# Gated attention and MLP on one core: the SBUF addresses of what TensorE reads

## The chip, the cores and the metric

One core of a Trainium2 chip runs the whole program. Its engines are TensorE (PE in the profile, with its weight loads apart as PEld), VectorE (DVE), ScalarE (ACT), GpSimd (POOL) and SyncE (SP), which issues the transfers here. The metric is the device time of one execution in microseconds, as the median of several runs. "Bytes modulo 512" below is the remainder of a tile's start address in its SBUF partition, the same in all 128 partitions.

## What is computed

Sequence 2048, width 512, 32 heads of 16, a causal window of 256 keys, an MLP of width 1792, and a gate that mixes both results:

```python
x = A_x                                            # [1, 2048, 512]
g = sigmoid((x * gate_w).sum(-1, keepdims=True))
qkv = x @ wqkv                                     # 32 heads of 16
p = softmax(where(0 <= i - j < 256, q @ k.T * 16 ** -0.5, -1e9))
a = (p @ v) @ wo
b = gelu(x @ w1 + b1) @ w2 + b2                    # tanh form
return g * a + (1 - g) * b
```

## The kernel before

The sequence is cut into NT = 4 tiles of T = 512 rows and 16 blocks of 128. Every dense product is made of three matmuls (`mm3`, L107 to L110): each operand is split into a high and a low part, and high by high, high by low and low by high are summed. Such a matmul reads 128 columns of weights and 512 columns of the other operand, in 4-byte elements.

The dense work is one generator, `dense()` (L896): `qkv(t)` for the four tiles (transposes of x at L261, then q and k at L294 and V at L334), `mlp(n)` for eight half-layers (first product "u", second product "y"), and `final(t)` (product "a" with `wo`).

Attention runs beside it from about 105 us on. For each unit of work the loop at L926 records: a matmul for the row maxima (L519, tile `sm`, weights from the stack `qd`, moving operand from the stack `kd`), one for the scores (L564, tile `st`, weights from the stack `ks`, moving operand from the stack `qs`), on every fourth block the products with V (L608, tiles `pv_st` and `pv_sm`, weights from `vbuf`, moving operand the probabilities `pt`), and then as much dense work as its estimate of the unit's time allows (`fill`, L907). So TensorE's queue alternates `sm`, `st` and about three dense matmuls. VectorE takes the row maxima (L524), ScalarE the exponentials (L586), GpSimd cuts the window's ends (L580) and writes the maxima into rows of `qs` (L546). The order of all five engines is written out by this loop (`manual_schedule`, L44), with a table of due times (`after`, L115); no scheduler moves anything afterwards. All transfers are issued by SP.

The tiles lie in SBUF in the order of their pools, and nearly fill it. From low to high addresses, with the start modulo 512 bytes:

| tiles | read by TensorE as | bytes modulo 512 |
|---|---|---|
| `qs`, `ks`, `qd`, `kd` (stacks of q and k, 16, 16, 16 and 12 KB) | scores and maxima; in `qkv(0)` to `qkv(2)` also x | 0 |
| `ident`, `x1`, `ya`, `xr` and other working tiles | transposes | 0 |
| `pt` (7 of 5 KB) | moving operand of L608 | 0 |
| `xt` (16 KB) | x of the MLP, x of `qkv(3)` | 0 |
| `w` (14 of 4 KB), `h` (7 of 4 KB) | weights and activations, high and low parts | 0 |
| `M`, `den`, `jm`, `b1c`, `cut`, `own`, `nil`, `nm` | `nil` only | various |
| `vbuf` (V, two halves, heads 68 bytes apart) | weights of L608 | 0 |

Inside a tile the matmuls start at multiples of 512 bytes, but for `qs` and `kd`, whose starts step by 64 columns (256 bytes), and `pt` (also 256). The stacks serve twice: `qkv_x` (L247) puts the transposed x of the tiles 0, 1 and 2 into the buffers of `ks`, `qd` and `qs` (L251 and L252), before attention needs them.

Of the kernel before, what the change touches and what calls it, by code (L numbers as in the profile page):

```python
# [9 lines left out]
F32 = mybir.dt.float32  # L10
F32R = mybir.dt.float32r
BF16 = mybir.dt.bfloat16
AF = mybir.ActivationFunctionType
ALU = mybir.AluOpType
# [3 lines left out]
S, D, F, H, DH, W = 2048, 512, 1792, 32, 16, 256  # L18
T = 512
NT = S // T  # L20
NB = T // 128
NC = D // 128
# [10 lines left out]
def gated_mix(ctx: ExitStack, tc: tile.TileContext, x, wqkv, wo, w1, b1, w2, b2, gate_w, out):  # L33
    nc = tc.nc
    x = x[0]
    out = out[0]

    cp = ctx.enter_context(tc.tile_pool(name="cp", bufs=1))
    sb = ctx.enter_context(tc.tile_pool(name="sb", bufs=1))
    cs = ctx.enter_context(tc.tile_pool(name="cs", bufs=1))  # L40
# [5 lines left out]
    def f32(ap):  # L46
        return ap.bitcast(F32)

    tt = cp.tile([128, 2 * RB, 32], F32, name="tt")
    mask = cp.tile([128, 320], BF16, name="mask")  # L50
    qs = cp.tile([128, 2, S], F32R, name="qs")
    ks = cp.tile([128, 2, 2, 2 * T], F32R, name="ks")
    qd = cp.tile([128, 2, 2, 2 * T], F32R, name="qd")
    kd = cp.tile([128, 2, 2, W + T], F32R, name="kd")

    idle = cs.tile([128, 320], BF16, tag="jm", bufs=1, name="idle")
    nc.gpsimd.memset(idle, 0.0)


    SQ = [dr.tile([H // NC, 16, 3, NC, T], F32, name=f"SQ{t}") for t in range(NT)]  # L60
# [12 lines left out]
    gwb = sb.tile([128, D], F32, tag="ya", bufs=2, name="gwb")  # L73
# [10 lines left out]
    for r in (0, 64):  # L84
        for e in (0, 1):
            v = cut[r:r + 64, e]
            nc.gpsimd.affine_select(out=v, in_=v, pattern=[[1 - 2 * e, 64]], compare_op=ALU.is_ge, fill=0.0,
                                    base=-e, channel_multiplier=2 * e - 1)

    own = cs.tile([128, 4], F32, name="own")  # L90
    nil = cs.tile([128, 1], F32, name="nil")
    nc.gpsimd.memset(nil, 0.0)
    nc.gpsimd.memset(own, 0.0)
    for s in (0, 1):
        for k in (0, 1):
            v = own[64 * s:64 * s + 4].rearrange("r (p s) -> r s p", s=2)[:, s]
# [1 line left out]
                                    fill=1.0, base=-k, channel_multiplier=1)  # L98
    nms = cs.tile([128, 2 * RB, 32], F32R, name="nm")
    nc.gpsimd.memset(f32(nms), 0.0)  # L100
    vbuf = cs.tile([128, 2, NB * 68 + 16], F32, name="vbuf")
    nc.gpsimd.memset(vbuf[:, :, NB * 68:], 0.0)
    z = cs.tile([128, S // 128], F32, name="z")
    g = cs.tile([128, S // 128], F32, name="g")
    g1 = cs.tile([128, S // 128], F32, name="g1")

# [8 lines left out]
    def after(ns, fn, *args):  # L115
        now[1] += 1
        heapq.heappush(todo, (now[0] + ns, now[1], fn, args))
# [7 lines left out]
    def tick(ns):  # L125
        now[0] += ns
        while todo and todo[0][0] <= now[0]:
            step_todo()
# [9 lines left out]
    def half_pt(name):  # L138

        if not spare:  # L140
            v = sb.tile([128, 2, 2, 320], F32, tag="pt", bufs=PTS, name=name)
            v = v.rearrange("p h a b -> p h (a b)")
# [104 lines left out]
    def qkv_x(t, b):  # L247

        if b == 0:
            if t < NT - 1:  # L250
                v = (ks.rearrange("p a b c -> p (a b c)"), qd.rearrange("p a b c -> p (a b c)"),  # L251
                     qs.rearrange("p a c -> p (a c)"))[t]  # L252
                v = v.rearrange("p (c s t) -> p c s t", c=NC, s=2)
            else:
                v = sb.tile([128, NC, 2, T], F32R, tag="xt", bufs=1, name=f"xt{t}")
            xts[t] = v
        xt = xts[t]
        xr = xrs[t, b]
        p = ps.tile([128, NC, 128], F32, tag="sm", bufs=3, name=f"xp{t}_{b}")
        for c in range(NC):  # L260
            nc.tensor.transpose(p[:, c], xr[:, c * 128:(c + 1) * 128], ident)  # L261
        tick(0 if t == 0 else 4 * 110)

        def hi():
            nc.scalar.activation(xt[:, :, 0, b * 128:(b + 1) * 128], p, AF.Copy)

        def lo():
            nc.vector.tensor_sub(xt[:, :, 1, b * 128:(b + 1) * 128], p,
                                 f32(xt[:, :, 0, b * 128:(b + 1) * 128]))
            done.add(("x", t, b))  # L270
        if t == 0:
            hi(), lo()
        else:
            after(100, hi), after(500, lo)

    def gate(t):
        for b in range(NB):
            after(1500 * b, gate_z, t, b)
        after(6500, gate_end, t)

    def gate_end(t):
        sl = slice(t * NB, (t + 1) * NB)
        nc.scalar.activation(g1[:, sl], z[:, sl], AF.Exp, scale=-1.0)
        nc.vector.tensor_scalar(g1[:, sl], g1[:, sl], 1.0, None, op0=ALU.add)
        nc.vector.reciprocal(g[:, sl], g1[:, sl])
        nc.vector.tensor_scalar(g1[:, sl], g[:, sl], -1.0, 1.0, op0=ALU.mult, op1=ALU.add)

    def gate_z(t, b):
        xr = xrs.pop((t, b))
        junk = sb.tile([128, D], BF16, tag="sq", bufs=2, name=f"xj{t}_{b}")  # L290
        nb = t * NB + b
        nc.vector.tensor_tensor_reduce(junk, xr, gwb, 1.0, 0.0, ALU.mult, ALU.add, z[:, nb:nb + 1])

    def qkv_qk(t, j):  # L294

# [198 lines left out]
    def load_qs(g_, c):  # L494
        ready(c, g_, 0)
        need(("v", NT - 2, NB - 1))
        for s in range(2):
            v = f32(qs[64 * s + 4:64 * s + 52, :, c * T:(c + 1) * T])
            nc.sync.dma_start(v, part(SQ[c], g_, s).rearrange("r (a c) -> r a c", a=2))
# [53 lines left out]
    def att_exp(g_, kb, i):  # L553
# [4 lines left out]
        if i == 0:  # L558
            pts[g_, kb] = sb.tile([128, 2, 2, 320], F32, tag="pt", bufs=PTS, name=f"pt{g_}_{kb}")
        pt = pts[g_, kb]  # L560
# [6 lines left out]
        n = 1 + (w == W + 64)  # L567
        late = g_ * NKB + kb >= NU - LEAD
        both = not late and kb % NB < NB - 1
# [22 lines left out]
    def att_pvs(u):  # L592

        g_, kb = divmod(u, NKB)
        c, k = divmod(kb, NB)
# [323 lines left out]

    NU = NG * NKB  # L920
    NQ = NG * NT
# [4 lines left out]
    for u in range(-LEAD, NU):  # L926
        m = u + LEAD
        gm, bm = divmod(m, NKB)
        step = STEP if u >= 0 else STEP0
        for i in range(4):  # L930
# [8 lines left out]
            for op, i in [(op, k) for k in pair for op in ORDER[:3]] + [("f", k) for k in pair]:  # L939
                if op == "s" and u >= 0:  # L940
                    att_exp(u // NKB, u % NKB, i)
                if op == "m" and m < NU:
# [5 lines left out]
        if m < NU and bm % RB == RB - 1:  # L948
            after(900, att_rows, gm, bm // RB)
        if m % NB == QAT % NB and QAT <= m < QAT + NKB:  # L950
            load_qs(0, (m - QAT) // NB)
# [18 lines left out]
WARM = (9, 4)  # L970
RB = 4
NKB = S // 128
PTS = 7
RAWS = 152000.0
PUT = 1200
# [44 lines left out]
```

## Time and profile before

| | |
|---|---|
| median of 3 runs | 750.84 us (750.7 to 752.2) |
| the profiled execution, its own time | 750.61 us |
| its span, from the first to the last instruction | 748.9 us |
| granted TensorE clock, mean | 1.000 |
| busy: PE, PEld, DVE, ACT, POOL | 98%, 81%, 70%, 56%, 50% |
| transfers | 172.12 MB, 230 GB/s over the span |

The table is from the page of the profile. Busy times of PE are those of overlapping matmuls: a matmul's recorded duration (about 0.39 us for 512 columns) is longer than the distance to the next one's start (0.23 us), since the next begins while the first drains. How much each matmul costs is therefore read from starts in the timeline, not from durations.

### The profile page before, as it was taken

The page shows a single profiled execution, that of the slowest core. Times are in us where ns is not written, and L with a number is a line of the kernel's source. Part 1 is how long each engine was busy: PE and PEld are TensorE (multiplying, and loading weights), DVE is VectorE, ACT ScalarE, POOL GpSimd, SP SyncE. Part 2 cuts the span into 40 slices and gives each one's busy share as a digit, 9 for nine tenths or more (in the row PEclk, how much of TensorE's full clock was granted, in tenths as well). Part 3 has the DMA queues.
Part 4 walks back from the last instruction along what each step waited for, and adds up shares of the span by engine and source line. Part 5 has one row for each costly group of instructions (what it writes and reads, how often), then busy time and mean ns, then how long its engine had stood idle before and what let it go on. Part 6 is the DMA issues. An engine that isn't in the chain of part 4 may idle for free.

```text
span 748.9 us, 17963 instructions
## 1 busy us (share of the span) xinstructions
PE 734.0 (98%) x6129; PEld 606.7 (81%) x6129; DVE 520.6 (70%) x1567; ACT 421.7 (56%) x972; POOL 372.4 (50%) x846
## 2 busy tenths in 40 slices
PE   9999999998999999999999999999999999999998
PEld 7888888876788888888887887888888888878787
DVE  4532325799768867986798689768867886784552
ACT  4434532358537845764695478447735853784541
POOL 4200000339756865876587567747765875630000
PEclk9999999999999999999999999999999999999999
DMA  9889798997995777799676989996799799438682
GB/s 316 329 268 407 257 392 277 273 312 182 273 251 133 172 229 211 176 227 249 164 174 152 241 215 230 259 235 155 171 268 244 180 238 239 136 88 262 217 287 106
DMA packets 179259, 172.12 MB, mean 230 GB/s; under 512 B 56672, under 2 KB 122976, under 8 KB 179168
## 3 DMA queue, kind: packets, MB, share of 16 engines
q1 hardware_dynamic: 179168, 170.97, 81.3%
q8 instruction: 49, 0.80, 0.5%
q14 instruction: 42, 0.34, 0.2%
HBM read 108.53 MB, written 62.39 MB: 228 GB/s over the span
## 4 chain that ended last, share of the span: by engine, by line
PE 84%; DMA 4%; DVE 4%; ACT 3%; issue 3%; SPq 1%; POOL 1%; DVEq 0%; ACTq 0%; POOLq 0%
PE sm L519 9%; PE st L564 8%; PE pv_sm L608 7%; PE y L108 6%; PE y L109 6%; PE y L110 6%; PE u L108 6%; PE u L109 5%; PE u L110 5%; PE qk L110 4%; PE qk L108 4%; PE qk L109 4%; PE pv_st L608 2%; PE a L108 2%; PE v L108 2%
## 5 line engine op out<-in xcount | busy, mean ns | idle before, releaser
L524 DVE CUSTOM_DVE_ANT_0 jm<-sm,mask 128x320 bf16<-128x320 f32 (+4 forms) x512 | 238.0, 465 | 95.6 <-PE sm L519 61.2
L580 POOL TENSOR_SCALAR_AFFINE_SELECT pt<-pt 64x256 f32<-64x256 f32 (+1 forms) x538 | 228.1, 444 | 108.6 <-ACT pt L586 98.1
L586 ACT ACTIVATE pt<-st 128x320 f32<-128x320 f32 (+4 forms) x512 | 199.6, 424 | 138.7 <-PE st L564 136.1
L519 PE MATMUL sm<-kd,qd 96*128 96x320 f32 (+4 forms) x512 | 154.1, 312 | 6.0 <-DVE M L524 5.1
L564 PE MATMUL st<-qs,ks 128*128 128x320 f32 (+4 forms) x512 | 154.4, 309 | 1.7 <-ACT pt L586 1.7
L546 POOL CAST qs<-tt 4x256 fp32r<-4x256 f32 x256 | 124.2, 485 | 52.7 <-DVE tt L539 42.0
L519 PEld LDWEIGHTS sm<-kd,qd 96*128 96x128 f32 x512 | 96.5, 188 | 32.8 <-DVE M L524 13.5
L564 PEld LDWEIGHTS st<-qs,ks 128*128 128x128 f32 x512 | 97.5, 190 | 18.5 <-ACT pt L586 2.9
L108 PE MATMUL y<-w,h 128*128 128x512 f32 x224 | 88.6, 395 | 0.0
L109 PE MATMUL y<-w,h 128*128 128x512 f32 x224 | 88.1, 393 | 0.0
L110 PE MATMUL y<-w,h 128*128 128x512 f32 x224 | 87.9, 393 | 0.0
L108 PE MATMUL u<-mx,w 128*128 128x512 f32 x196 | 80.0, 408 | 0.0
L109 PE MATMUL u<-mx,w 128*128 128x512 f32 x196 | 77.4, 395 | 0.0
L110 PE MATMUL u<-mx,w 128*128 128x512 f32 x196 | 77.1, 393 | 0.0
L608 PE MATMUL pv_st<-pt,vbuf 64*32 64x320 f32 (+4 forms) x1408 | 73.3, 346 | 1.5 <-ACT pt L586 1.0
L608 PE MATMUL pv_sm<-pt,vbuf 64*32 64x320 f32 (+4 forms) x1408 | 74.2, 347 | 0.2
L608 PEld LDWEIGHTS pv_sm<-pt,vbuf 64*32 64x32 f32 x1408 | 51.2, 106 | 19.3 <-issue 2.2
L325 DVE TENSOR_TENSOR qke<-qk,qke 128x512 fp32r<-128x512 f32 x32 | 22.0, 689 | 46.9 <-ACT qke L322 31.1
L322 ACT ACTIVATE qke<-qk 128x512 fp32r<-128x512 f32 x32 | 19.1, 598 | 56.2 <-PE qk L110 30.3
L110 PEld LDWEIGHTS y<-w,h 128*128 128x128 f32 x224 | 42.1, 188 | 9.8
L608 PEld LDWEIGHTS pv_st<-pt,vbuf 64*32 64x32 f32 x1408 | 46.2, 106 | 1.8 <-ACT pt L586 1.1
L338 POOL MEMSET vx<- 128x32 f32 x16 | 2.4, 155 | 88.9 <-DMA SK<-qke 30.7
(148 smaller groups left out, 1334.7 us busy)
## 6 DMA issues: line engine op xcount, KB each, us to landing
kd<-SK SPq DMA_DIRECT2D x32, 384.0 KB
qs<-SQ SPq DMA_DIRECT2D x64, 192.0 KB
mx<-XT SPq DMA_DIRECT2D x24, 512.0 KB
SQ<-qke SPq DMA_DIRECT2D x16, 512.0 KB
SK<-qke SPq DMA_DIRECT2D x16, 512.0 KB
ND<-nd SPq DMA_DIRECT2D x32, 256.0 KB
raw_w<-in_B_w_dram SPq DMA_DIRECT2D x28, 256.0 KB
ks<-SK SPq DMA_DIRECT2D x32, 192.0 KB
```

Source lines behind the costliest of these rows:

```text
L108: nc.tensor.matmul(p, lh, rh, start=first, stop=False)
L109: nc.tensor.matmul(p, lh, rl, start=False, stop=False)
L110: nc.tensor.matmul(p, ll, rh, start=False, stop=last)
L322: nc.scalar.activation(e[:, h], p, AF.Copy)
L325: nc.vector.tensor_sub(e[:, 1 - h], p, f32(e[:, h]))
L519: nc.tensor.matmul(p[:, :w], qd[0:96, n, pr, 128 * j:128 * (j + 1)], kd[0:96, n, pr, k1 - w:k1], start=True, stop=True)
L524: nc.vector.tensor_tensor_reduce(junk[:, :w], p[:, :w], mask[:, 320 - w:320], 1.0, -3e38, ALU.add, ALU.max, M[:, 2 * (b % RB) + hb, pr:pr ...
L546: nc.gpsimd.tensor_copy(dst, src.unsqueeze(1).broadcast_to([4, 2, RB, 32]))
L564: nc.tensor.matmul(p[:, :w], ks[:, slot(g_, kb // NB), pr, at:at + 128], qs[:, pr, k0:k0 + w], start=True, stop=True)
L580: nc.gpsimd.affine_select(out=v, in_=v, pattern=[[0, v.shape[1]], [1 - 2 * e, 64]], compare_op=ALU.is_ge, fill=0.0, base=-e, channel_multi ...
L586: nc.scalar.activation(pt[:, hf, pr, :w], p[:, :w], AF.Exp, scale=SCALE)
L608: nc.tensor.matmul(pv[r // 64][32 * i:32 * i + 32, q - c * T:e - c * T], vts[g_, b // NB][r:r + 64, v:v + 32], rhs(r), start=start, stop=s ...
```

## The change

The four stacks become views of one tile `stk`, in the order `kd`, `ks`, `qd`, `qs`, with 32 elements (128 bytes) more at its end. Every tile allocated after it moves up by 128 bytes. `vbuf` is allocated directly after `idle`, at a multiple of 512 bytes again. x of the first three tiles stands in the buffers of `ks`, `qd` and `qs` as before, but 128 bytes later in each, so its end reaches 128 bytes into the next buffer. Room for the 128 bytes comes from `own` and `nil`, now one tile `small`, and from `z`, whose sums now stand in `g`.

```diff
-    qs = cp.tile([128, 2, S], F32R, name="qs")
-    ks = cp.tile([128, 2, 2, 2 * T], F32R, name="ks")
-    qd = cp.tile([128, 2, 2, 2 * T], F32R, name="qd")
-    kd = cp.tile([128, 2, 2, W + T], F32R, name="kd")
+    nk, nx = 4 * (W + T), 8 * T
+    stk = cp.tile([128, nk + 3 * nx + SHIFT], F32R, name="stk")
+    kd = stk[:, 0:nk].rearrange("p (n u x) -> p n u x", n=2, u=2)
+    ks, qd = (stk[:, nk + i * nx:nk + (i + 1) * nx].rearrange("p (n u x) -> p n u x", n=2, u=2) for i in (0, 1))
+    qs = stk[:, nk + 2 * nx:nk + 3 * nx].rearrange("p (u x) -> p u x", u=2)
+
+    def x_view(i):
+        v = stk[:, nk + i * nx + SHIFT:nk + (i + 1) * nx + SHIFT]
+        return v.rearrange("p (c s t) -> p c s t", c=NC, s=2)
...
+    vbuf = cs.tile([128, 2, NB * 68 + 16], F32, name="vbuf")
...
-    own = cs.tile([128, 4], F32, name="own")
-    nil = cs.tile([128, 1], F32, name="nil")
+    small = cs.tile([128, 5], F32, name="small")
+    own, nil = small[:, 0:4], small[:, 4:5]
...
-    vbuf = cs.tile([128, 2, NB * 68 + 16], F32, name="vbuf")
...
-    z = cs.tile([128, S // 128], F32, name="z")
...
-                v = (ks.rearrange("p a b c -> p (a b c)"), qd.rearrange("p a b c -> p (a b c)"),
-                     qs.rearrange("p a c -> p (a c)"))[t]
-                v = v.rearrange("p (c s t) -> p c s t", c=NC, s=2)
+                v = x_view(t)
...
-        nc.scalar.activation(g1[:, sl], z[:, sl], AF.Exp, scale=-1.0)
+        nc.scalar.activation(g1[:, sl], g[:, sl], AF.Exp, scale=-1.0)
...
-        nc.vector.tensor_tensor_reduce(junk, xr, gwb, 1.0, 0.0, ALU.mult, ALU.add, z[:, nb:nb + 1])
+        nc.vector.tensor_tensor_reduce(junk, xr, gwb, 1.0, 0.0, ALU.mult, ALU.add, g[:, nb:nb + 1])
...
+SHIFT = 32
```

The instructions of each engine, their shapes and their order are the same in both programs; their addresses differ. The waits are the same too, except that the first copy of maxima into `qs` (L546 on GpSimd) waits for TensorE at two points of its progress in turn, the later of which it waited for before. Modulo 512 bytes, the stacks and `vbuf` now start at 0, and `ident`, x in all its buffers, `pt`, `w`, `h` and the working tiles at 128.

## The prediction

> **What bounds the kernel now.** I read the page first, then the stages, then single starts in the timeline. The page and the table of stages (columns: length of the stretch, busy time and count of PE, PEld, DVE, ACT and POOL, clock, share of the 16 transfer engines, GB/s):
>
> ```profile
> span 748.9 us, 17963 instructions
> PE 734.0 (98%) x6129; PEld 606.7 (81%) x6129; DVE 520.6 (70%) x1567; ACT 421.7 (56%) x972; POOL 372.4 (50%) x846
> 16.00:105.00 89.00, 89.00 (x414) 73.37 (x413) 34.35 (x70) 37.90 (x91) 5.89 (x16) 1.00 0.91 330
> 105.00:190.00 85.00, 81.19 (x446) 66.09 (x444) 63.85 (x204) 43.12 (x105) 35.35 (x63) 1.00 0.93 275
> 190.00:400.00 210.00, 208.12 (x1994) 174.19 (x1994) 164.83 (x538) 131.13 (x303) 144.14 (x335) 1.00 0.79 201
> ```
>
> TensorE is never without work for long, at the full granted clock (1.00), and no other engine is above 70%. Only between 105 and 190 us does it lose some 4 us, and there the transfer engines are busiest. So the time is the sum of what TensorE's matmuls cost, and a change of addresses matters if it alters the distance between two starts. That distance is read where nothing else runs, in the last product:
>
> ```profile
> 738.37 0.39 PE L110 MATMUL a<-wo,ot 128*128 128x512 f32 x1
> ...
> 742.45 0.39 PE L110 MATMUL a<-wo,ot 128*128 128x512 f32 x1
> ...
> 743.03 0.28 PE L108 MATMUL a<-wo,ot 128*128 128x256 f32 x1
> ...
> 745.43 0.28 PE L110 MATMUL a<-wo,ot 128*128 128x256 f32 x1
> ```
>
> Between the first two rows lie 18 distances: 4.08 / 18 = 227 ns for 512 columns. Between the last two lie 20: 2.40 / 20 = 120 ns for 256. The difference gives (227 - 120) / 256 = 0.417 ns a column, so 213 and 107 ns are the streaming itself and **13 ns come on top of each matmul**, whatever its length. Beside attention it is a little more:
>
> ```profile
> 503.21 0.39 PE L109 MATMUL u<-mx,w 128*128 128x512 f32 x1
> 503.44 0.40 PE L110 MATMUL u<-mx,w 128*128 128x512 f32 x1
> 503.68 0.31 PE L519 MATMUL sm<-kd,qd 96*128 96x320 f32 x1
> 503.82 0.31 PE L564 MATMUL st<-qs,ks 128*128 128x320 f32 x1
> 503.98 0.39 PE L108 MATMUL u<-mx,w 128*128 128x512 f32 x1
> ```
>
> Here 512 columns take 230 to 240 ns and 320 columns (133 ns of streaming) 140 to 160 ns. One reads also that a dense matmul before `sm` (503.44 to 503.68) is no dearer than one before another dense one, within the 10 ns that the timeline resolves. The products with V behave otherwise. Each starts in groups of eight:
>
> ```profile
> 403.35 0.44 PE L608 MATMUL pv_st<-pt,vbuf 64*32 64x320 f32 x2
> ...
> 403.61 0.38 PE L608 MATMUL pv_st<-pt,vbuf 64*32 64x256 f32 x2
> ...
> 403.83 0.38 PE L608 MATMUL pv_st<-pt,vbuf 64*32 64x256 f32 x2
> ```
>
> A group takes 260 ns for 320 columns and 220 ns for 256; at two column times per element the streaming alone would be 267 and 213 ns. So eight weight loads add almost nothing. V's heads start 68 bytes apart, hence mostly not where the moving `pt` starts modulo 512.
>
> **The change part by part.** No instruction is added, removed or moved on any engine, so every term is a price that depends on an address.
>
> *Handovers between dense work and the stacks.* While a matmul streams, the weights of the next one are loaded. After the change these two reads differ by 128 bytes modulo 512 in two kinds of places: a dense matmul followed by `sm` or `st`, and `sm` or `st` followed by a dense one. In the program's order these are 374 and 361 places, 735 together; the cap from the profile is each of the attention matmuls once in and once out:
>
> ```profile
> L564 PE MATMUL st<-qs,ks 128*128 128x320 f32 x448 | 139.4, 319 | 0.7 <-ACT pt L586 0.7
> L519 PE MATMUL sm<-kd,qd 96*128 96x320 f32 x448 | 138.6, 321 | 4.5 <-DVE M L524 4.2
> L564 PEld LDWEIGHTS st<-qs,ks 128*128 128x128 f32 x512 | 97.5, 190 | 18.5 <-ACT pt L586 2.9 <-issue 0.8 <-ACT sqh L728 0.2
> L519 PEld LDWEIGHTS sm<-kd,qd 96*128 96x128 f32 x512 | 96.5, 188 | 32.8 <-DVE M L524 13.5 <-issue 3.0 <-DVE nd L632 0.9
> ```
>
> If the 13 ns are two reads that meet in the same place, up to 13 ns can go at each: 735 x 13 ns = 9.6 us. If they are a fixed price, nothing goes; if the new offset makes the reads meet where they did not, the same 9.6 us could be added. The rows of V are the nearest ones that have unequal starts, and say that most can go; but their loads are 32 columns wide and their stream runs at half the rate. The rows of `sm` and `st` have the right shape and the offset of 256 bytes in about half of them (`qs` and `kd` step by 64 columns), and show 140 to 160 ns for all, so an offset alone need not help. I take a third: 735 x 4.4 ns = **3.2 us less**, all of it on TensorE's own path, where nothing hides it. What follows on the other engines moves up with TensorE; VectorE at 70% has room.
>
> [...] The 13 ns are seen in the rows above; whether they are a collision no row here can show.
>
> *Dense on dense, and stack on stack.* w, h and x in all its buffers move together, and the stacks stay together: 1758 and 632 places keep their difference. I cost them at nothing; if absolute position counted, 1758 places at 1 ns would be 1.8 us either way.
>
> *V against `pt`.* The loads already differ in start and add almost nothing: nothing to win. Eight loads hidden in 267 ns could at worst come to cost their 13 ns once per group: the rows of L608 are
>
> ```profile
> L608 PE MATMUL pv_sm<-pt,vbuf 64*32 64x320 f32 x512 | 42.0, 430 | 0.0
> L608 PEld LDWEIGHTS pv_sm<-pt,vbuf 64*32 64x32 f32 x1408 | 51.2, 106 | 19.3 <-issue 2.2 <-DVE nm L536 1.4 <-DVE tt L539 0.8
> ```
>
> 2816 in both tiles make 352 groups, 4.6 us at most. I take nothing.
>
> *Transfers.* All that DMA writes into or reads from the shifted tiles now starts 128 bytes later in SBUF. In most stages this is covered by TensorE, which is 100% busy between 16 and 105 us beside a share of 0.91. It is not covered between 105 and 190 us: the chain of waits there holds two transfers into `qs`, behind a full queue.
>
> ```profile
> 159.80 5.81 DMA qs<-SQ
> 165.63 2.87 SPq L170
> 169.02 4.79 DMA qs<-SQ
> ```
>
> The transfers into `qs` themselves stay at multiples of 512 in SBUF; what stands ahead of them (weights, x, stores of q and k) is shifted. [...] I take 0.2 us more.
>
> *The rest.* The first copy into `qs` ends its wait at the same point of TensorE's progress as before. `z` in `g`, `own` with `nil` and the one tile for four stacks change names alone. Nothing.
>
> Sum: the profiled execution took 750.61 us, 1.7 us around its span of 748.9, and the median of the runs is 750.84. 750.6 - 3.2 + 0.2 = 747.6 against the execution, 747.8 against the median. I say **747.7 us**.
>
> **The rivals.**
>
> 1. *Nothing happens* (750.8). The 13 ns are a fixed price of such a matmul. For it: `sm` and `st` at 256 bytes of difference cost what they cost at 0, and handovers cost what dense pairs cost. Against it: the V groups, which load eight times and pay almost nothing.
>
> [...]
>
> 3. *The handovers become dearer.* The reads of a stack and of dense data, now 128 bytes apart, meet more often than at equal starts: the same 735 places at 4 to 13 ns, 753.7 to 760.4, say 756. For it: no row shows that a difference of 128 is better than none. Against it: the V groups again.
>
> **How the numbers follow.** The handovers becoming cheaper: 0.44, with times from 742 (nearly all of the 13 ns) to 749. Nothing: 0.21. Transfers dearer: 0.20. Handovers dearer: 0.15. About 0.2%, 1.5 us, is what a measurement of this kernel can tell from no change. A gain under 1.5 us takes 0.04 from the first case, and a loss under it 0.03 from the second rival: faster 0.41, within 0.2% 0.27, slower 0.32. The range leaves out more than 10 ns saved at each handover and more than 7 ns lost: 735 x 10 ns = 7.3 and 735 x 7 ns = 5.1 us from 750.8, so 743.5 to 756. The likeliest case's own range is 743 to 749.
>
> **What would show it.** If right, 512 columns before `sm` take about 5 ns less in the timeline beside attention than 512 columns before dense work, `st` before dense work is under 150 ns, the three matmuls of the last product stay at 227 ns, and the gain is spread evenly over 120 to 690 us, none before and none after. If nothing happens, all distances stay. If transfers are dearer, the share between 16 and 190 us rises and the stall at 158 to 174 us is longer while distances stay. What would make it wrong at once is a change in the dense pairs, or in the last product, which I cost at nothing.

## The result and the profile after

The changed kernel takes **753.33 us** (median of 13 runs, 751.46 to 756.45); the kernel before takes 750.84 (13 runs beside them, 749.63 to 753.0). The ratio is 1.0032, with a 95% interval of 1.0019 to 1.0044: slower by 0.3%, or 2.4 us, where 747.7 was forecast. (Ratios are not the quotients of the medians beside them, here and below, and differ from these by up to 0.1%.) The time lies inside the range, the direction is wrong.

In the changed program L112 to L114 are the lines L108 to L110 of before, L521 is L519, L566 is L564 and L610 is L608, and all four stacks carry the name `stk`. The profiled execution took 751.97 us. From its page:

```profile
span 750.3 us, 17963 instructions
PE 734.8 (98%) x6129; PEld 607.2 (81%) x6129; DVE 520.4 (69%) x1567; ACT 422.3 (56%) x972; POOL 371.7 (50%) x846
q1 hardware_dynamic: 179168, 170.97, 82.5%
L521 PE MATMUL sm<-stk 96*128 96x320 f32 (+4 forms) x512 | 154.8, 314 | 7.4 <-DVE M L526 6.7
```

The same number of instructions as before, and the same busy times within 1 us on every engine. Of the idle time ahead of `sm`, 6.7 us end with a row maximum on VectorE. The view of waits before has (us in total, times, longest)

```profile
PE sm L519 <- DVE M L524: 5.1, 10, 1.0
```

and after

```profile
PE sm L521 <- DVE M L526: 6.7, 11, 2.0
```

so the longest of them takes 2.0 us in place of 1.0; it is the one near 162 us, which took 0.65 us before. The table of stages (columns as in the prediction):

```profile
16.00:105.00 89.00, 89.00 (x414) 73.36 (x413) 34.42 (x70) 37.94 (x91) 5.87 (x16) 1.00 0.92 332
105.00:190.00 85.00, 80.79 (x444) 65.90 (x443) 62.25 (x201) 42.75 (x104) 33.74 (x61) 1.00 0.95 271
190.00:400.00 210.00, 208.02 (x1993) 174.07 (x1992) 164.58 (x539) 131.21 (x305) 143.82 (x334) 1.00 0.79 201
```

Before 105 us nothing moves: TensorE is at 89.00 of 89.00 again. Between 105 and 190 us it is busy for 0.4 us less than before, and the share of the transfer engines is 0.95 in place of 0.93. A fixed window understates that loss, because less work falls into it: counted from matmul to matmul, from the one that starts at 105.0 us in the profile of before to the one at 190.0, 444 distances later, the stretch takes 84.97 us before and 86.35 after. After that no stage shows anything by itself: TensorE is busy all the time whether a matmul costs 230 ns or 232.

The price of a place is therefore read between two landmarks that are far apart, with no single wait between them. I take the start of the first product with V of a block, near 233 us and again twelve such products later, and near 472 us and thirteen later. Between the first two lie 1956 matmuls, between the last two 2091. The timeline of before (start, duration, instruction):

```profile
232.51 0.24 PE L608 MATMUL pv_sm<-pt,vbuf 64*32 64x64 f32 x1
...
435.13 0.24 PE L608 MATMUL pv_sm<-pt,vbuf 64*32 64x64 f32 x1
...
471.99 0.24 PE L608 MATMUL pv_sm<-pt,vbuf 64*32 64x64 f32 x1
...
685.66 0.24 PE L608 MATMUL pv_sm<-pt,vbuf 64*32 64x64 f32 x1
```

and of the changed kernel:

```profile
233.89 0.24 PE L610 MATMUL pv_sm<-pt,vbuf 64*32 64x64 f32 x1
...
436.92 0.24 PE L610 MATMUL pv_sm<-pt,vbuf 64*32 64x64 f32 x1
...
473.98 0.24 PE L610 MATMUL pv_sm<-pt,vbuf 64*32 64x64 f32 x1
...
688.10 0.24 PE L610 MATMUL pv_sm<-pt,vbuf 64*32 64x64 f32 x1
```

435.13 - 232.51 = 202.62 us before and 203.03 after; 213.67 before and 214.12 after. Each stretch is longer by 0.4 us, evenly, at a clock of 1.00. Outside attention nothing has changed. The last product of the changed kernel reads

```profile
738.58 0.39 PE L112 MATMUL a<-wo,ot 128*128 128x512 f32 x1
...
743.79 0.39 PE L114 MATMUL a<-wo,ot 128*128 128x512 f32 x1
```

23 distances in 5.21 us, 227 ns as before.

So the spans of the two profiles, 1.4 us apart, come out like this. Summed over all pairs of successive starts whose distance is within 60 ns of before's, the changed kernel is **1.04 us** longer. What is left, 0.3 us, is single waits of TensorE that moved: 1.3 us more near 162 us, 1.1 us less near 694. The medians are a further 1.1 us apart; the experiments below ask whether that is the change's, too.

### The profile page after: what moved, and what is told of

Read it like the earlier page. It is cut to its first block, busy times and chain, and to the rows that moved or that the text cites. A ratio compares the mean times of both kernels' runs of the same rounds, so it can differ in the third digit from the quotient of the medians.

```text
span 750.3 us, 17963 instructions
## 1 busy us (share of the span) xinstructions
PE 734.8 (98%) x6129; PEld 607.2 (81%) x6129; DVE 520.4 (69%) x1567; ACT 422.3 (56%) x972; POOL 371.7 (50%) x846
## 3 DMA queue, kind: packets, MB, share of 16 engines
q1 hardware_dynamic: 179168, 170.97, 82.5%
## 4 chain that ended last, share of the span: by engine, by line
PE 83%; DMA 5%; DVE 4%; ACT 3%; issue 3%; POOL 1%; SPq 1%; DVEq 0%; ACTq 0%; POOLq 0%
PE sm L521 9%; PE st L566 8%; PE pv_sm L610 7%; PE y L112 6%; PE y L114 6%; PE y L113 6%; PE u L112 5%; PE u L114 5%; PE u L113 5%; PE qk L114 4%; PE qk L112 4%; PE qk L113 4%; DMA stk<-SK 2%; PE a L112 2%; PE v L114 2%
## 5 line engine op out<-in xcount | busy, mean ns | idle before, releaser
L521 PE MATMUL sm<-stk 96*128 96x320 f32 (+4 forms) x512 | 154.8, 314 | 7.4 <-DVE M L526 6.7
L566 PE MATMUL st<-stk 128*128 128x320 f32 (+4 forms) x512 | 153.6, 308 | 0.7 <-ACT pt L588 0.7
L548 POOL CAST stk<-tt 4x256 fp32r<-4x256 f32 x256 | 124.2, 485 | 52.7 <-DVE tt L541 42.1
L521 PEld LDWEIGHTS sm<-stk 96*128 96x128 f32 x512 | 96.3, 188 | 33.8 <-DVE M L526 14.8
L566 PEld LDWEIGHTS st<-stk 128*128 128x128 f32 x512 | 97.7, 191 | 17.7 <-ACT pt L588 1.7
L112 PE MATMUL y<-w,h 128*128 128x512 f32 x224 | 88.7, 396 | 0.0
L114 PE MATMUL y<-w,h 128*128 128x512 f32 x224 | 88.2, 394 | 0.0
L112 PE MATMUL u<-mx,w 128*128 128x512 f32 x196 | 79.9, 408 | 0.0
L114 PE MATMUL u<-mx,w 128*128 128x512 f32 x196 | 77.5, 395 | 0.0
L610 PE MATMUL pv_st<-pt,vbuf 64*32 64x320 f32 (+4 forms) x1408 | 73.3, 346 | 1.5 <-ACT pt L588 1.0
L610 PE MATMUL pv_sm<-pt,vbuf 64*32 64x320 f32 (+4 forms) x1408 | 74.2, 346 | 0.1
L610 PEld LDWEIGHTS pv_sm<-pt,vbuf 64*32 64x32 f32 x1408 | 51.1, 106 | 19.3 <-issue 2.3
L114 PEld LDWEIGHTS y<-w,h 128*128 128x128 f32 x224 | 42.1, 188 | 10.0
L610 PEld LDWEIGHTS pv_st<-pt,vbuf 64*32 64x32 f32 x1408 | 46.1, 106 | 1.9 <-ACT pt L588 1.1
```

The source lines that it names most:

```text
L112: nc.tensor.matmul(p, lh, rh, start=first, stop=False)
L114: nc.tensor.matmul(p, ll, rh, start=False, stop=last)
L521: nc.tensor.matmul(p[:, :w], qd[0:96, n, pr, 128 * j:128 * (j + 1)], kd[0:96, n, pr, k1 - w:k1], start=True, stop=True)
L548: nc.gpsimd.tensor_copy(dst, src.unsqueeze(1).broadcast_to([4, 2, RB, 32]))
L566: nc.tensor.matmul(p[:, :w], ks[:, slot(g_, kb // NB), pr, at:at + 128], qs[:, pr, k0:k0 + w], start=True, stop=True)
L610: nc.tensor.matmul(pv[r // 64][32 * i:32 * i + 32, q - c * T:e - c * T], vts[g_, b // NB][r:r + 64, v:v + 32], rhs(r), start=start, stop=s ...
```

## The experiments

Three theories stood against each other. **A, transfers:** data that starts 128 bytes past a multiple of 256 moves more slowly, so TensorE waits longer where it waits for loads. **B, handovers:** a matmul whose weights start elsewhere, modulo 256 bytes, than the operand that streams meanwhile costs more. **C, the rest:** the new order of tiles and the merged ones, apart from the 128 bytes. The figures of all profiles stand in one table at the end of this section.

**The new layout without the 128 bytes.** Against the changed kernel:

```diff
+    cs.tile([128, 32], F32, name="pad")
     vbuf = cs.tile([128, 2, NB * 68 + 16], F32, name="vbuf")
-SHIFT = 32
+SHIFT = 0
```

> The new order of the stacks in one tile, the merged small tiles, and no shift: all starts are multiples of 512 as before. Theory A and theory B: ratio 1.000, 750.8 us. Theory C (order of the stacks, the one tile or the small tiles): ratio 1.003 as in the change.

751.5 us against 751.15, ratio 1.0004 (0.9991 to 1.0016). The landmarks of its timeline:

```profile
232.70 0.24 PE L611 MATMUL pv_sm<-pt,vbuf 64*32 64x64 f32 x1
...
435.33 0.24 PE L611 MATMUL pv_sm<-pt,vbuf 64*32 64x64 f32 x1
```

202.63 us, as before the change. C falls as far as this measurement reaches, 0.16% at most: the loss comes with the 128 bytes.

**All tiles 128 bytes past, stacks too.** The shift is kept for all that the change moves, and a pad ahead of the stacks moves these as well; V stands behind `g`. No two reads of TensorE then differ in start that agreed before, while every transfer into the stacks is shifted besides. Against the changed kernel:

```diff
+    cp.tile([128, SHIFT], F32R, name="pad")
-    stk = cp.tile([128, nk + 3 * nx + SHIFT], F32R, name="stk")
+    stk = cp.tile([128, nk + 3 * nx], F32R, name="stk")
...
-        v = stk[:, nk + i * nx + SHIFT:nk + (i + 1) * nx + SHIFT]
+        v = stk[:, nk + i * nx:nk + (i + 1) * nx]
...
-    vbuf = cs.tile([128, 2, NB * 68 + 16], F32, name="vbuf")
...
+    g = cs.tile([128, S // 128], F32, name="g")
+    vbuf = cs.tile([128, 2, NB * 68 + 16], F32, name="vbuf")
...
-    g = cs.tile([128, S // 128], F32, name="g")
```

It ran twice, the second time beside the changed kernel on one chip.

> The stacks, V and all the rest lie 128 bytes past a multiple of 512: every difference between two reads of TensorE is as in the kernel before, every transfer is shifted in SBUF as in the change, those into the stacks too. Theory A (transfers that start late are dearer): at least as slow as the change, ratio 1.003 or more, share of q1 at or above 82.5%. Theory B (the handovers between stacks and dense work are dearer): ratio 1.000, 750.8 us.

> All starts 128 bytes past a multiple of 512 once more. Theory A: ratio 1.001 to 1.003 again, share of q1 near 87%, the loss before 16 us, at 158 to 176 us and at the end; theory B alone: 1.000. Distances from 190 to 690 us as in the kernel before, in both.

752.54 against 751.15, ratio 1.0019 (1.0006 to 1.0032), then 752.79 against 751.27, ratio 1.0009 (0.9995 to 1.0023). Timeline and page of the second:

```profile
233.98 0.24 PE L611 MATMUL pv_sm<-pt,vbuf 64*32 64x64 f32 x1
...
436.54 0.24 PE L611 MATMUL pv_sm<-pt,vbuf 64*32 64x64 f32 x1
```

```profile
q1 hardware_dynamic: 179168, 170.97, 86.2%
```

The landmarks are 202.56 us apart: with all starts equal again, the distances are those of before, although everything is displaced. So it is the difference that costs, as B says, and not the place. B alone would leave this kernel at the time of before. It is slower by 0.2% in the first measurement, clear of the noise, and by 0.1% in the second, not clear of it; so A is not refuted. The transfer engines are busy for 86 to 87% of the span in place of 81 to 82%, and TensorE's 81st matmul starts at 16.1 to 16.2 us where all the others have it at 14.9 to 15.5. The chain that ended last shows where: it runs through the first load of weights (start, time to landing), here of before, of the change and of this kernel's first profile:

```profile
3.69 5.07 DMA raw_qk<-in_A_wqkv_dram
3.69 5.56 DMA raw_qk<-in_A_wqkv_dram
3.69 6.52 DMA raw_qk<-in_A_wqkv_dram
```

In all profiles whose chain holds this load, it takes 5.0 to 5.4 us where its target starts at a multiple of 512 bytes (six profiles), 5.5 to 5.9 where it starts 128 bytes later (the five of the change, and one of the kernel "x with the stacks" below) and 6.5 to 6.6 in the two of this kernel. So a shifted load, among others that are under way, does land later. Why it takes 1 us more here than in the change, where it is shifted by as much, is open.

**The other way round.** The stacks and V 128 bytes past a multiple of 256, all else at multiples of 512. The differences are those of the change, the transfers shifted are the others. Against the changed kernel:

```diff
-    nc = _bacc.Bacc("TRN2", target_bir_lowering=False, num_devices=1, dynamic_dma_scratch_size=256)
+    nc = _bacc.Bacc("TRN2", target_bir_lowering=False, num_devices=1, dynamic_dma_scratch_size=128)
```

With the smaller buffer every tile is meant to sink by 128 bytes. A trace lists no addresses, but this one's fits: the share of the transfer engines is 86.0%, near the 86.9 and 86.2% of the kernel above, where the loads into the stacks are shifted too, and not 81 to 83% as in all others. Beside it the changed kernel ran once more, unaltered.

> The mirror image of the change: the stacks and V lie 128 bytes past a multiple of 256 and all else lies at multiples of 512, so that the handovers between stacks and dense work read at unequal starts as in the change, while weights, x and stores are aligned and only the loads into the stacks are shifted. Theory B (handovers): TensorE's distances grow as in the change, 1.0 us from 190 to 690 us; theory A (transfers): distances are those of the kernel before, and what is lost stands in single waits at 158 to 176 us and at the end. If both count: 1.0 us in the distances and a ratio of 1.001 to 1.003.

> The change once more. Theory B: its distances from 190 to 690 us are again 1.0 us longer in sum than before, to 0.1 us, since they don't depend on the run; theory A: they differ from run to run. Ratio 1.002 to 1.004 in either.

753.75 against 751.27, ratio 1.0026 (1.0012 to 1.0040), and for the change 754.1, ratio 1.0030 (1.0015 to 1.0044). Between the landmarks 202.98 us in both, 0.4 more than with equal starts. Sums over the distances: 0.89 us more than before, and 1.10 for the change. B's term is the same from either side.

**x with the stacks.** Only x of the first three tiles goes back to a multiple of 512 bytes, so that it differs from `w` in the dense work before attention. Against the changed kernel:

```diff
-        v = stk[:, nk + i * nx + SHIFT:nk + (i + 1) * nx + SHIFT]
+        v = stk[:, nk + i * nx:nk + (i + 1) * nx]
```

> The change, with x of the first three tiles at the start of the stacks' buffers: x at 0 and its weights at 128 bytes modulo 512, and the stores of x start at multiples of 512. Theory A: a little faster than the change, ratio 1.002 to 1.003. Theory B (dearer by unequal starts): some 480 more dense pairs at unequal starts, at 3 ns each 1.4 us more, ratio 1.005, with the dense matmuls between 16 and 105 us further apart than 227 ns.

753.58 against 751.15, ratio 1.0031 (1.0017 to 1.0044). The timeline near 40 us, the product that makes V, in this kernel:

```profile
40.13 0.39 PE L114 MATMUL v<-v,stk 128*128 128x512 f32 x1
...
43.62 0.40 PE L114 MATMUL v<-v,stk 128*128 128x512 f32 x1
```

and in the changed one:

```profile
40.15 0.40 PE L114 MATMUL v<-v,stk 128*128 128x512 f32 x1
...
43.55 0.39 PE L114 MATMUL v<-v,stk 128*128 128x512 f32 x1
```

15 distances in 3.49 us are 233 ns each with unequal starts; in 3.40 us, 227 ns with equal ones. Over the 486 distances from about 15 to 120 us it adds up to 1.9 us. The time does not show it. In the profile part of the 1.9 us comes off the distance with the wait near 162 us, in the stretch where transfers already held TensorE back (1.21 us against 2.30). B holds, and dense pairs would have paid if x had not been moved along with `w`.

**w against everything else.** No shift, but `w`, `h` and the squares 128 bytes past x, the stacks and V. Against the changed kernel:

```diff
-SHIFT = 32
+SHIFT = 0
...
+            sb.tile([128, 32], F32, tag="pad", bufs=1, name="pad")
```

> All starts are multiples of 512 as before, but the tiles w and h, and the two behind them, lie 128 bytes further: every dense matmul of q, k, V and of the MLP's first product has the two reads at unequal starts, some 1150 places, while the stacks, x and the raw weights are aligned. Theory B: 4 to 6 ns at each, 5 to 7 us in TensorE's distances, ratio 1.006 to 1.009. Theory A: few transfers are shifted (stores from h), distances as before, ratio 1.000 to 1.001.

754.73 against 751.12, ratio 1.0051 (1.0033 to 1.0069). A loss of 3.6 us, the largest of all, but below what was expected. It is all in the distances, which add up to 3.57 us more than before in the profile. The part before 120 us came in full, 2.0 us, nearly all of it over 418 unequal pairs, 4.6 ns each. Beside attention, from landmark to landmark, it is only 0.5 us (203.09) and another 0.5 (214.20 against 213.67). That is not a price of the dense pairs: the 331 of the MLP's first product in these two stretches, which read at unequal starts, keep their distance to 0.1 ns in the mean. The largest parts stand between `sm` and `st`, which start alike (0.32 and 0.25 us), and where `st` is followed by the second product (0.18 and 0.15). Why the dense pairs that read at unequal starts pay nothing there, these runs do not tell.

**The reads alone.** A kernel with nothing on TensorE but chains of 36 matmuls from two tiles, whose starts are set; after them, transfers alone. The core of it, with `m` and `w` the offsets of stream and weights in elements:

```python
for c, m, w in (("a", 0, 0), ("b", 0, 32), ("c", 32, 0), ("d", 32, 32), ("e", 0, 64), ("f", 0, 16), ...):
    for k in range(36):
        at = 128 * (k % 4) + w
        nc.tensor.matmul(p, wt[:, at:at + 128], mv[:, m:m + 512], start=k == 0, stop=k == 35)
```

> None of the reference is computed: runs of 36 matmuls alone, 512 and 320 columns wide, with the weights and the moving operand at chosen starts modulo 512 bytes (a: 0 and 0, b: weights at 128, c: moving at 128, d: both at 128, e: weights at 256, f: weights at 64, g: weights at 32, h: moving at 32 and weights at 16), then loads and stores of 16 times 256 KB at starts of 0, 128 and 256 bytes. Theory A: all matmul distances equal (227 and about 147 ns), loads or stores at 128 slower by 5 to 12% than at 0 and 256. Theory B: distances of b or c differ from a and d by 2 to 13 ns, loads and stores all alike. If the distances are alike and the transfers too, the slowdown needs both running together.

The timeline, one row for each chain of 36 (start, length of the chain):

```profile
17.39 8.33 PE L42 MATMUL far_a<-mv,wt 128*128 128x512 f32 x36
25.55 8.53 PE L42 MATMUL far_b<-mv,wt 128*128 128x512 f32 x36
33.92 8.55 PE L42 MATMUL far_c<-mv,wt 128*128 128x512 f32 x36
42.31 8.37 PE L42 MATMUL far_d<-mv,wt 128*128 128x512 f32 x36
50.52 8.33 PE L42 MATMUL far_e<-mv,wt 128*128 128x512 f32 x36
58.68 8.56 PE L42 MATMUL far_f<-mv,wt 128*128 128x512 f32 x36
...
93.81 5.44 PE L47 MATMUL near_c<-mv 128*128 128x320 f32 x36
99.09 5.43 PE L47 MATMUL near_d<-mv 128*128 128x320 f32 x36
104.36 5.44 PE L47 MATMUL near_e<-mv 128*128 128x320 f32 x36
```

From start to start, over 36: equal starts (a) 8.16 / 36 = 227 ns; weights 128 bytes further (b) 232.5; the stream 128 bytes further (c) 233; both (d) 228; weights 256 bytes further (e) 227, as if equal. That is B in its plainest form: **a difference of 128 bytes, modulo 256, adds 6 ns to 512 columns**. At 320 columns (where every matmul loads the same weights) all starts give the same 147 ns. The prediction's 13 ns on top of the streaming stay at equal starts: they are no collision that any of these offsets removes.

Of the transfers, loads of 16 times 256 KB took 13.8 to 14.8 us with a start of 128 bytes and 13.6 to 15.1 with 256: no price. Stores of as much, each closed by a marker on ScalarE that waits for them (bracket), 256, 0, 128 and 256 bytes past:

```profile
166.22 0.23 ACT L63 ACTIVATE bank<-mark 128x16 f32<-128x16 f32 x1 [11.61 <-DMA out_dram<-bank]
178.30 0.23 ACT L63 ACTIVATE bank<-mark 128x16 f32<-128x16 f32 x1 [11.85 <-DMA out_dram<-bank]
190.65 0.23 ACT L63 ACTIVATE bank<-mark 128x16 f32<-128x16 f32 x1 [12.12 <-DMA out_dram<-bank]
202.07 0.23 ACT L63 ACTIVATE bank<-mark 128x16 f32<-128x16 f32 x1 [11.20 <-DMA out_dram<-bank]
```

From row to row 12.1 us for 0, 12.4 for 128 and 11.4 for 256. These times hold the pause between two sets as well, about 1.7 us ahead of a set at 0, 1.3 ahead of one at 128 and none ahead of one at 256, so they settle nothing. The durations of the single packets of 2 KB, which the trace has too, do: in the mean of a set 84 ns at 0 and 256, 86.5 to 87.2 at 128. **A store that starts 128 bytes late in SBUF is dearer by 3 to 4%**, here with no other transfer under way.

**More offsets alone.** The same with twelve starts of the weights, with 256 columns, with narrower weights, and with units of five in the manner of attention (three of 512 columns, two of 320).

> None of the reference is computed: runs of 36 matmuls of 512 columns with the moving operand at 0 and weights at 0, 16, 32, 64, 96, 128, 192, 224, 240, 256, 384 and 512 bytes (far a to l), 256 columns with weights at 0 and 128 (half), weights of 64 and 32 columns (slim), and the kernel's unit of three dense matmuls and two of 320 columns with equal starts (unit a) and with the 320s and their weights 128 bytes further (unit b); then loads in pieces of 512 bytes and stores of 2 KB at 0, 128 and 256. If unequal starts modulo 256 are what costs: 227 ns at 0, 256 and 512, about 233 at 32 to 224, none below 227; unit b 3 to 9 ns longer than unit a per five matmuls. If the 13 ns on top of the streaming come from the weight load, slim takes less than 227. If late starts make transfers dearer: loads in 512-byte pieces at 128 slower than at 0 and 256 by 5% or more.

```profile
18.56 8.32 PE L43 MATMUL far_a<-mv,wt 128*128 128x512 f32 x36
26.72 8.33 PE L43 MATMUL far_b<-mv,wt 128*128 128x512 f32 x36
34.89 8.55 PE L43 MATMUL far_c<-mv,wt 128*128 128x512 f32 x36
...
117.97 4.47 PE L48 MATMUL half_a<-mv,wt 128*128 128x256 f32 x36
122.28 4.44 PE L48 MATMUL half_b<-mv,wt 128*128 128x256 f32 x36
126.56 8.43 PE L53 MATMUL slim_a<-mv,wt 128*64 128x512 f32 x36
134.83 8.50 PE L53 MATMUL slim_b<-mv,wt 128*32 128x512 f32 x36
143.17 7.26 PE L60 MATMUL unit_a<-mv,wt 128*128 128x512 f32 x36
150.26 7.35 PE L60 MATMUL unit_b<-mv,wt 128*128 128x512 f32 x36
```

At 0 and 16 bytes (rows a and b) a matmul of 512 columns takes 227 ns, also at 240, 256 and 512; at 32 (row c) 233, and 229 to 234 at 64, 96, 128, 192, 224 and 384. No start beats equal ones. With 256 columns there is no price (120 ns at 0, 119 at 128). Weights of 64 and 32 columns are not cheaper to load in passing: 230 and 232 ns, so the 13 ns do not scale with the load. The chain in units (b less a) is 0.09 us longer for its 7 units, 13 ns a unit, where the kernel shows about 3. In this mixture the distances of 320 columns grow too, from 144 and 145 ns to 147 and 149, and that of the dense matmul ahead of them shrinks from 236 to 231: a delay does not stay with the pair that reads at unequal starts.

Loads in pieces of 512 bytes took 8.1 to 8.4 us 128 bytes past a multiple, and 7.9 to 8.7 at 256: again no price, alone. (At 0 they took 11.3 to 11.7 us, but there each set starts some 1.8 us after the last packet of the set before, and the others at once.) Their packets take 28 to 30 ns at all three starts. Stores took 12.3 to 13.7 us at 128, 12.1 at 0 and 11.4 at 256, and their packets again 84 ns at 0 and 256 and 86.5 to 87.2 at 128.

**More profiles, for the waits.** 1.04 us is less than half of the loss. Five further single profiles show how the rest scatters: two of the kernel before, three of the change; a sixth is of the layout without the shift. One more run of the kernel before, beside the last four, took 755.29 us at a mean granted clock of 0.998, longer than any of these.

> The kernel before, profiled again: how much the single waits at 158 to 182, 204, 443 and 694 us differ between two executions of one kernel. Theory B: distances the same to 0.1 us over 190 to 690 us, the waits by up to 2 us. If the waits of the kernel before repeat as well, the 1 to 1.8 us in them in the change belong to the change.

> As the look before it, a third profile of the kernel before.

> The change, profiled again, for the sum of the single waits at 162, 204, 443 and 694 us (2.7, 4.3 and 3.8 us in three profiles of the kernel before, 3.0 and 5.7 in two of the change). If the shifted transfers lengthen them: 4 us and more in most looks, and stretches of lower granted clock behind the longest. If they don't: 2.5 to 4.5 us as before. The distances are 0.40 and 0.45 us longer than before in the two stretches without waits, in either case.

> The change once more: single waits over 4 us in sum if the shifted transfers lengthen them, 2.5 to 4.5 us if not; distances 0.40 and 0.45 us longer than before in either case.

> The change once more: single waits over 4 us in sum if the shifted transfers lengthen them, 2.5 to 4.5 us if not; distances 0.40 and 0.45 us longer than before in either case.

> All starts at multiples of 512, profiled again: single waits of 2 to 4.5 us in sum as in the kernel before, no stretch of lower clock, distances as before.

The distances come out the same each time. The single waits do not: in the change they add up to 2.96, 5.71, 2.64, 5.11 and 3.82 us, mean 4.05; in the kernel before and the layout without the shift to 2.65, 4.25, 3.74, 2.17 and 2.30, mean 3.02. With a scatter (standard deviation) of 1.3 and 0.9 us in the two sets of five, the difference of 1.0 us is not settled.

The stretch from 105 to 190 us says more than the four waits. The change needs 85.4 to 87.1 us for it, mean 86.4; the five profiles with all starts at multiples of 512 need 85.0 four times and 86.3 once, mean 85.3. The steady distances in it are the same to 0.1 us. So about 1.1 us of the loss stands there, in waits and in what follows them; five against five with one exception make it likely, not certain. It is the stretch for which the prediction says that transfers are not covered by TensorE.

A wait can bring something after it. The fourth profile of the change, in the timeline (the bracket is the wait ahead of the instruction) and in windows:

```profile
162.23 0.30 PE L566 MATMUL st<-stk 128*128 128x320 f32 x1
164.68 0.42 PE L521 MATMUL sm<-stk 96*128 96x320 f32 x1 [2.14 <-DVE M L526]
...
165.14 0.63 PE L112 MATMUL u<-xt,w 128*128 128x512 f32 x1
165.57 0.63 PE L113 MATMUL u<-xt,w 128*128 128x512 f32 x1
```

```profile
162.30:164.90 2.60, 0.46 (x3) 0.23 (x2) 1.89 (x4) 2.04 (x5) 1.26 (x1) 1.00 1.05 393
164.90:168.30 3.40, 3.40 (x11) 2.81 (x11) 3.26 (x12) 1.82 (x4) 1.15 (x2) 0.51 0.99 282
```

After an idle time of 2.14 us the granted clock is 0.51 for 3.4 us, and 512 columns take 430 ns in place of 227 to 240: here a wait is followed by a loss beyond its own length. The length of the wait alone does not decide (names as in the table below). The first profile of "all past" has the same halving behind 1.97 us, the second of the change has one (0.51 from 181.2 to 184.0 us) behind waits of 0.64 and 0.45 us, and the first of the change and the second of before have none behind 1.99 and 2.04.

How often it happens differs between the layouts. A halved stretch of 3.4 us lowers a run's mean clock by 0.5 x 3.4 / 750 = 0.0023. A mean of 0.998 or less is listed for 5 of 71 timed runs of the kernel before and of the layout without the shift, for 8 of 25 of the change, for 14 of 36 of the two layouts that shift the loads into the stacks ("all past" and "stacks past"), and for none of 11 of the last two. Such runs of the change are 2.1 to 2.3 us longer than its others. As an estimate from these figures, (8/25 - 5/71) x 2.2 us = 0.5 us of the change's loss. In the three profiles that have a halved stretch, it lies between 105 and 190 us, so this is a part of the 1.1 us above, not an addition to it.

**All profiles.** "First" and "second" are the stretches between the landmarks; "early" is the sum over the 486 distances from about 15 to 120 us; "to 190" is the stretch from 105 to 190 us, from matmul to matmul as above; the four waits are TensorE's distances at 162, 204, 443 and 694 us, where 0.23 (0.09 for the last) is no wait; all in us. Medians with a ratio are from timed runs, the others are one run.

| kernel | first | second | early | to 190 | four waits, sum | transfers' share | time, ratio |
|---|---|---|---|---|---|---|---|
| before | 202.62 | 213.67 | 105.13 | 84.97 | 2.65 | 81.3% | 750.84 |
| before, second profile | 202.61 | 213.64 | 105.19 | 86.34 | 4.25 | 82.2% | 752.21 |
| before, third | 202.60 | 213.60 | 105.13 | 85.02 | 3.74 | 81.8% | 751.3 |
| layout, no shift | 202.63 | 213.53 | 105.15 | 85.04 | 2.17 | 80.8% | 751.5, 1.0004 |
| layout, no shift, second | 202.62 | 213.68 | 105.16 | 84.98 | 2.30 | 81.9% | 750.3 |
| all past | 202.57 | 213.65 | 105.14 | 86.58 | 4.17 | 86.9% | 752.54, 1.0019 |
| all past, again | 202.56 | 213.66 | 105.18 | 85.30 | 3.23 | 86.2% | 752.79, 1.0009 |
| the change | 203.04 | 214.12 | 105.13 | 86.35 | 2.96 | 82.5% | 753.33, 1.0032 |
| the change, again | 202.98 | 214.04 | 105.19 | 87.10 | 5.71 | 81.4% | 754.1, 1.0030 |
| the change, third | 203.00 | 214.06 | 105.13 | 85.38 | 2.64 | 81.9% | 751.96 |
| the change, fourth | 202.94 | 214.09 | 105.17 | 86.90 | 5.11 | 82.4% | 754.91 |
| the change, fifth | 203.02 | 214.08 | 105.13 | 86.11 | 3.82 | 82.6% | 752.59 |
| stacks past | 202.98 | 214.06 | 105.17 | 85.75 | 4.88 | 86.0% | 753.75, 1.0026 |
| x with the stacks | 203.04 | 214.10 | 107.00 | 85.48 | 4.09 | 82.0% | 753.58, 1.0031 |
| w past | 203.09 | 214.20 | 107.12 | 86.14 | 3.01 | 81.8% | 754.73, 1.0051 |

In the first column seven profiles with equal starts lie within 202.56 to 202.63 and eight with unequal ones within 202.94 to 203.09: the two groups do not touch. This is the clearest result of the study, and it is 0.4 us in 203.

The share of the transfer engines has two groups as well: 86 to 87% in the three profiles in which the loads into the stacks are shifted, 81 to 83% in all others. The packets show where it comes from: those of 512 bytes take 43 to 44 ns in the mean of a whole profile in the first group, 37 to 39 in the second, and those of 2 KB 100 to 103 in both.

No layout of the scan is cheaper than equal starts, and the kernel before has them wherever 512 columns stream while the weights of a dense product or of a stack are loaded. So the runs point to no version that beats it.

## Why the prediction was wrong

**The step that failed is the handovers**: "I take a third: 735 x 4.4 ns = 3.2 us less". The runs put 1.04 us more in its place, 1.4 ns for each of the 735 places. So the term had the wrong sign. (A second one, the transfers, was too small; it stands below.) The premise of the handovers was that the 13 ns might be two reads that meet, which an offset would part. Alone on TensorE the 13 ns are there at equal starts and at 512 columns grow (to 19) or stay with an offset; they do not shrink with narrower weights either. The argument from the nearest row failed with it. The V groups have unequal starts and eight cheap loads, but they stream at half the rate, in rows of 320 and 256 columns (269 and 216 ns for a group of eight, in the mean of the profile of before: 0.83 ns a column against 0.417), and chains of such widths show nothing of the price even alone. The rows of `sm` and `st`, 256 bytes apart in half of their places and no cheaper, were named as the row of the right shape and then outweighed. They were the right witness for another reason: 256 bytes counts as equal (227 ns in the chains, as at 0). By kind of pair, the change has 1.8 ns more from a dense start to `sm` (344 pairs), 3.1 from `sm` to `st` (408), 2.8 less from `st` to `sm` (112), 0.8 more from `st` to dense (290) and 0.4 less between dense ones (1689). Inside a unit the delay thus shows up ahead of `st`, where both stacks start alike; which of the reads causes it is not told apart.

**The first rival, by which this term is nothing, came nearer in size**: 750.8 us. Where 256 or 320 columns stream in uniform chains, the runs agree with it (120 and 119 ns, and 147 whatever the starts). At 512 columns they do not: 227 ns with equal starts, 233 with the weights 128 bytes off the stream.

**The third rival, handovers dearer, had the sign and the place right**, and its price was mis-sized: 4 to 13 ns at 735 places, 2.9 to 9.6 us, measured as 1.0. Uniform chains show the price at 512 columns only. If it were so in the kernel, only the 374 places from dense work into a stack would have it, and by the 6 ns measured alone that is 2.2 us as an estimate; the kernel shows half of it, and the chain in units alone twice as much. What a mixture of widths costs is thus measured, not explained. It had the smallest chance because of the V groups, the same wrong row.

**Dense on dense, stack on stack, V against `pt`: nothing.** By the kinds of pairs above, stack on stack is dearer by 1.0 us and dense on dense cheaper by 0.7, though their starts keep their difference; the delays move inside a unit, so only the unit as a whole is a clean measure. That position as such costs nothing is right: the landmarks with equal differences and shifted places ("all past") agree with before to 0.1 us, and the last product stays at 227 ns. V against `pt` is right, too: the mean distance between two products with V is that of before to 0.1 ns. That dense on dense is nothing before attention hangs on x being moved along: with x left behind it is 1.9 us.

**Transfers: 0.2 us more.** No run shows these 0.2 us. They are too little, as far as the profiles show, and this part stays open. Of the 2.4 us, 1.0 is shown as distances, and about 1.1 stands in the stretch from 105 to 190 us, where the distances do not change. That shifted transfers are dearer is shown: the first load of weights lands later (5.5 to 5.7 us against 5.0 to 5.4), stores by themselves take 3 to 4% more for each packet, and packets of 512 bytes take 43 to 44 ns in place of 37 to 39 where the loads into the stacks are shifted. That these delays are what lengthens the stretch is argued, not shown: the loads into the stacks, which TensorE's chain runs through there, are not shifted in the change. Loads by themselves took no longer at 128 bytes than at 256 (13.8 to 14.8 us against 13.6 to 15.1). Of what was to show dearer transfers, the share rises a little, from 0.91 to 0.92 before 105 us and from 0.93 to 0.95 up to 190, and the stretch to 190 us is longer, by 1.4 us in the first profile of the change and by 1.1 in the mean of five against five; one profile of the kernel before has it too. The distances were to stay in that case and grew by 1.0 us.

**The rest: nothing.** Right, by the layout without the shift. In the chances, the parts give 0.40, 0.28 and 0.32 for faster, the same and slower, not 0.41, 0.27 and 0.32.

**What was to show it.** The forecast of a gain spread evenly over 120 to 690 us had the place of the distances right: they do change there, evenly, and nowhere else. The sign is the other, and what the stretch to 190 us loses beside them was not in it.

## What to carry to other kernels

A fixed part of a matmul's cost, worked out from two lengths, does not say that anything collides; before a layout is changed for it, run the one instruction by itself at a few offsets, which here took two kernels. Keep the weights and the stream of long matmuls at the same start modulo 256 bytes (here 227 ns against 233 for 512 columns), and when one of them has to move, move its partner too (with everything moved, the landmarks stayed 202.56 us apart). Where a difference of some tenths of a per cent is to be explained, compare stretches between landmarks that hold no wait, since a single span here scatters by more than the effect. A stretch with waits takes several profiles of each kernel: here one profile of the kernel before lost as much there as those of the change.

## What the runs showed of the hardware

- The price of unequal starts has a step: none for 16 and 240 bytes, 2 to 7 ns from 32 to 224, none at 256 and 512, 6 again at 384. In uniform chains it is seen at 512 columns of 4-byte elements (227 ns against 229 to 234), not at 256 (120 and 119) or 320 (147).
- 320 columns have a distance of 147 ns alone, 133 of streaming and 13 on top, the same 13 as for 512 and 256.
- Weights of 64 and 32 columns make a matmul of 512 columns dearer, 230 and 232 ns against 227.
- The granted clock fell to 0.51 for 3.4 us behind a wait of 2.14 us, and 512 columns then took 430 ns. It did so behind 1.97 us in another profile, and not behind 1.99 and 2.04 in two more.
- The transfer engines' busy share rises from 81-83% to 86-87% where the loads into the stacks start 128 bytes late; packets of 512 bytes then take 43 to 44 ns in place of 37 to 39. Loads in pieces of 512 bytes by themselves took 28 to 30 ns a packet at all starts.
- Stores of 2 KB rows take 86.5 to 87.2 ns a packet where they start 128 bytes past a multiple of 256 in SBUF, and 84 at 0 and at 256.
